# Two small loads on another queue, other PSUM banks for one step's scores, and twenty identity transposes at the start of a fused attention and MLP kernel

## The chip, the cores and the metric

The kernel runs on one core of a Trainium2 chip. The metric is device time in microseconds (us) of one launch, lower is better; the time of a version is the median of several runs.

## The reference

Attention with a threshold, then an MLP with a squared ReLU, all in fp32. What matters of it:

```python
q, k, v: (8, 8, 576, 64)    tau = 0.02    w_in: (512, 2048)   w_out: (2048, 512)
scores = 0.125 * np.matmul(q, k.transpose(0, 1, 3, 2))
thresh = np.max(scores, axis=-1, keepdims=True) - tau
scores = np.where(scores >= thresh, scores, -1000000000.0)
scores = scores - np.max(scores, axis=-1, keepdims=True)
attn = np.exp(scores)
attn = attn / (np.sum(attn, axis=-1, keepdims=True) + 1e-09)
attn_out = np.matmul(attn, v)
x = attn_out.transpose(0, 2, 1, 3).reshape(4608, 512)
h = x @ w_in
r = np.maximum(h, 0.0)
return (r * r) @ w_out
```

## The kernel before, in words

Heads are handled in pairs, because two heads of 64 columns fill the 128 rows of TensorE. A *visit* is one pair of heads of one batch, and a visit is a row of *steps*; a step handles one block of 128 queries of both heads (u = 0 and u = 1). The first visits have two steps each: steps 0 and 1 belong to visit 0, steps 2 and 3 to visit 1, and so on. All engines are scheduled by hand: each engine and each queue does its instructions in the order in which the program writes them. One loop over the steps writes that order, and it spreads pieces of the MLP (attention output times `w_in`, square, times `w_out`) between the attention work of the steps, as soon as enough of the attention output is there. Before that, in the first steps, the attention chain has the engines nearly alone.

At the start, `load_qk(0)` loads the keys and queries of visit 0 in pieces of 32 partitions: four pieces of `kl`, four of `ql`, on the queues of SyncE (SP) and ScalarE (ACT) in turn. Keys m = 2 and m = 3 come in two parts, a large one (16 blocks, L173) and a small one (2 blocks, 8 KB, L175). The small ones are in the same queue as the large one. Then SP issues `load_qk(1)` (into tile `wo`, a part of which serves as a buffer until the weights of the second MLP layer come), the values `load_v(0)` and the first three pieces of weights, `load_weights(0..2)`. The DMAs of SP and ACT share eight completion semaphores in rotation: a ninth one waits until the first has landed, and so on. GpSimd (POOL) meanwhile makes the identity `ident`, issues the load of `tau` (L57), and clears a few tiles (L79, L236). VectorE (DVE) begins with the scaling of `tau` into `ntau8` (L58), and behind it in its order are the transposes `prep(0)` of L226 that make `qT` and `kT` from `ql` and `kl`.

One step s then consists of:

- `scores(s)`: TensorE multiplies `qT` by `kT` (L247), four matmuls of 288 columns (each two records in the trace), two for each head, into the PSUM tiles `s0` and `s1` (two banks each); DVE takes the row maxima (L269, two instructions).
- `turn(s - 2, ...)`: nine transposes on TensorE (L326) turn the finished weights of the step two before, three into one of the four tiles `bank4` to `bank7` (one PSUM bank each); ScalarE copies each three out to `wT` (L327).
- `exponents(s)`: ScalarE makes bias and threshold (L277, L278) and two exponentials out of `s0` and `s1` (L280).
- in the last step of a visit `prep` of the next visit: `qT` and `kT` again (L226, DVE); in other steps DVE has parts of the rounding of a weight piece (L140, L141, L144).
- `mix(...)`: from step 3 on, the weights `wT` times the values (L428).
- `threshold(s)`: DVE compares the scores with the threshold and multiplies (L292, two instructions), then sum and reciprocal (L294, L295).
- `divide(s)`: GpSimd scales the weights (L300, L302).

Every step takes its scores from the same `s0` and `s1`:

```python
sc = [psum.tile([P, 2, 512], FP32, tag=f"s{u}", name=f"s{u}") for u in range(n)]
```

So the matmuls of step s may begin when `threshold(s - 1)`, the last reader of `s0` and `s1`, is done with each of them. The four tiles of `bank` are first used by `turn(0, ...)` in step 2.

Of the kernel before, what the change touches and what calls it, by code (L numbers as in the profile page):

```python
# [9 lines left out]
FP32 = mybir.dt.float32  # L10
U32 = mybir.dt.uint32
AF = mybir.ActivationFunctionType
ALU = mybir.AluOpType
# [6 lines left out]
def kernel(  # L20
# [10 lines left out]
    nc = tc.nc  # L31
    B, H, S, D = q.shape
    d_model, d_ff = moe_w_in.shape
    n_tokens = out.shape[0]
    P = 128
# [10 lines left out]
    SCALE = 0.125  # L46
# [5 lines left out]
    psum = ctx.enter_context(tc.tile_pool(name="psum", bufs=1, space=bass.MemoryType.PSUM))  # L52

    ident = const.tile([P, P], FP32, name="ident")
    make_identity(nc, ident)
    ntau8 = const.tile([P, 1], FP32, name="ntau8")
    nc.gpsimd.dma_start(out=ntau8, in_=tau.to_broadcast([P, 1]))  # L57
    nc.vector.tensor_scalar(out=ntau8, in0=ntau8, scalar1=-1.0 / SCALE, scalar2=None, op0=ALU.mult)  # L58

    w_in_sb = const.tile([P, NMC, d_ff], FP32, name="w_in_sb")  # L60

# [14 lines left out]

    vs = [const.tile([P, 2 * NBLK + 2, D], FP32, name=f"vs{i}") for i in range(2)]
    qmid = const.tile([P, P], FP32, name="qmid")
    nc.gpsimd.memset(qmid, 0.0)  # L79
    at = RAW * 2 * WP  # L80
    w_slots = [const.tile([P, 2, S], FP32, name=f"w{i}") for i in range(2)]
    w_slots.append(spare[:, at:at + 2 * S].rearrange("p (u k) -> p u k", u=2))
# [16 lines left out]
    p5s = const.tile([P, HD], FP32, name="p5s")  # L99
    u_sum = const.tile([P, HD], FP32, name="u_sum")  # L100
    osb = const.tile([P, 2, d_model], FP32, name="osb")
    bank = {i: psum.tile([P, 512], FP32, tag=f"bank{i}", name=f"bank{i}") for i in range(4, 8)}


    n_in = d_ff // WP * NMC
# [18 lines left out]
    def load_weights(i):  # L124
        nc.sync.dma_start(out=weight_area(i).bitcast(mybir.dt.int64), in_=weight_piece(i)[0])
# [25 lines left out]
    def rows_of(n):  # L151
        return rows_in[n % 2 if n <= 2 * HP else 0]
# [3 lines left out]
    def rows_32(t, n, m):  # L156

        b, h = divmod(visits[n][0], HP)
        return t[b, 2 * h + m // 2, :, (m % 2) * 32:(m % 2) * 32 + 32].rearrange("(c p) d -> p c d", p=32)

    def load_qk(n):


        if by_dma(n):
            load_part(k, n)
            load_part(q, n)
            return
        for x, t in ((rows_of(n)[1], k), (rows_of(n)[0], q)):
            for m in range(4):
                src, to = rows_32(t, n, m), x[m * 32:(m + 1) * 32, :, :]  # L170
                queue = nc.scalar if n == 0 and m % 2 else nc.sync
                last = REST // 32 if t is k and m >= 2 else 0
                queue.dma_start(out=to[:, last:, :], in_=src[:, 0:S // 32 - last, :])  # L173
                if last:
                    queue.dma_start(out=to[:, 0:last, :], in_=src[:, S // 32 - last:, :])  # L175

    def load_part(t, n):
        x = rows_of(n)[0 if t is q else 1]
        loads.extend((x[m * 32:(m + 1) * 32, :, :], rows_32(t, n, m)) for m in range(4))
# [31 lines left out]
    def prep(n):  # L211

        prep_part(q, n)
        prep_part(k, n)
# [8 lines left out]
    def prep_part(t, n):  # L223
        to, rows = (qT, rows_of(n)[0]) if t is q else (kT[n % 2], rows_of(n)[1])
        arrived(rows)
        nc.vector.transpose(to, rows.rearrange("p c d -> p (c d)"))  # L226
# [5 lines left out]
    LITTLE = 2.0 ** -20  # L232

    stats = [const.tile([P, 8, 2], FP32, name=f"st{i}") for i in range(4)]
    for st in stats:
        nc.gpsimd.memset(st[:, 4, :], S * LITTLE)  # L236
    weights = {}

    def scores(s):


        vis, i = steps[s]
        n = 2 if i < NBLK or paired(vis) else 1
        sc = [psum.tile([P, 2, 512], FP32, tag=f"s{u}", name=f"s{u}") for u in range(n)]

        def term(u, half, rows, lhsT, keys, to=slice(0, P)):
            nc.tensor.matmul(sc[u][to, half, 0:HALF], lhsT, keys[rows, half * HALF:(half + 1) * HALF],  # L247
                             start=True, stop=True)

        if i == NBLK and paired(vis):  # L250
            for half in range(2):
                for v_ in range(2):
                    for u in range(2):
                        rows, cols = slice(u * D, (u + 1) * D), slice(v_ * D, (v_ + 1) * D)
                        term(u, half, rows, qmid[rows, cols], kT[v_], cols)
        elif i == NBLK:
            for half in range(2):
                term(0, half, slice(0, P), qmid, kT[vis % 2])
        else:
            halves = [(half, u) for half in range(2) for u in range(n)]  # L260
            if early():
                halves.sort(key=lambda x: x[1])
            for half, u in halves:
                rows = slice(u * D, (u + 1) * D)
                term(u, half, rows, qT[rows, i * P:(i + 1) * P], kT[vis % 2])
        st = stats[s % len(stats)]
        mx = st[:, 0, 0:n]
        for u in range(n):
            nc.vector.tensor_reduce(out=mx[:, u:u + 1], in_=sc[u][:, :, 0:HALF], axis=AX.XY, op=ALU.max)  # L269

        w = w_slots[(s - first_dma) % (2 if by_dma(vis) else 3)][:, 0:n, :]
        weights[vis, i] = w, sc, st

    def exponents(vis, i):
        w, sc, st = weights[vis, i]
# [305 lines left out]
    def paired(n):  # L581

        return n >= 3 * HP
# [8 lines left out]
    def by_dma(n):  # L592

        return n >= 3 * HP - 1
# [31 lines left out]
    def early():  # L626
        return state["step"] < min(chunk_at)
# [10 lines left out]
    def add_chunk(j):  # L638
        waiting.extend(pieces_of(j))
# [40 lines left out]
    for s, (n, i) in enumerate(steps):  # L680
        if s < HP * FIRST:
            x = int(n > 0 and i == 0)
        else:
            x = 2 if n >= 2 * HP and i == NBLK else 1
# [46 lines left out]
            prep_at[d].append(lambda n=nxt: prep_part(k, n + 1))  # L731

    load_qk(0)
    load_qk(1)
    load_v(0)
    for i in range(RAW):
        load_weights(i)
    prep(0)
    done = 0
    rounded_by = [0]  # L740
    for s in range(END + 1):
        state["step"] = s
        state["usable"] = rounded_by[-1]
        rounded_by.append(state["rounded"])
        on = s < NST
        now = []
        if on:
            n, i = steps[s]
            at = visits[n][1].index(i)
            last = at == len(visits[n][1]) - 1  # L750
            now = list(range(done, done + pieces[s]))
            done += pieces[s]
            more = n + 1 < len(visits)
            short = n < 2 * HP
            if short and at == 0 and 0 < n + 1 < 2 * HP:
                load_qk(n + 2)
            elif not short and at == 1 and not by_dma(n):
                load_qk(n + 1)
            if now:
                round_weights(now[0], 0)  # L760
            scores(s)
        old = steps[s - 2] if 2 <= s < NST + 2 and not by_dma(steps[s - 2][0]) else None
        at_once = now or old or early()
        lay = on and last and more and not by_dma(n)
        if old:
            turn(*old, 0)
            turn(*old, 1)
        if on:
            exponents(n, i)
            if at == 1:  # L770
                split_left(n)
            if lay:
                prep(n + 1)
            elif now:
                round_weights(now[0], 1)
        if s in mixes and not old:
            mix(*mixes[s])
            for j in chunk_at.get(s, ()):
                add_chunk(j)
        quarter = rate(s) / 4 if s < END else 1e9  # L780
        fill(quarter)
        if s in mixes and old:
            mix(*mixes[s])
            for j in chunk_at.get(s, ()):
                add_chunk(j)
        if old:
            turn(*old, 2)
        state["free"] = s > first_dma
        if on:
            threshold(n, i)  # L790
            for fn in prep_at[s] + load_at[s]:
                fn()
            if lay and now:
                round_weights(now[0], 1)
            if now:
                round_weights(now[0], 2)
                round_weights(now[0], 3)
            if not at_once:
                divide(n, i)
        if 0 < s <= NST and by_dma(steps[s - 1][0]):  # L800
            m, x = steps[s - 1]
            turn_blocks(m, x)
        for what in place_at[s]:
            place_blocks(*what)
        some_loads()
        fill(quarter)
        some_loads()
        if on and at_once:
            divide(n, i)
        fill(quarter)  # L810
        some_loads()
        fill(quarter)
        some_loads()
        if on:
            if now:
                end_rounding(now[0])
            for p in now[1:]:
                for stage in range(4):
                    round_weights(p, stage)
                end_rounding(p)  # L820
            if at == 0 and 0 < n <= 2 * HP:
                load_v(n)
            elif last and n >= 2 * HP and not by_dma(n):
                load_v(n + 1)
# [35 lines left out]
```

## Time and profile before

| | |
|---|---|
| median of 7 runs | 1414.63 us (1411.81 to 1415.89) |
| the profiled execution's own time | 1411.81 us |
| its span, first to last instruction | 1410.0 us |
| TensorE busy | 1359.4 us, 96% of the span |
| VectorE, GpSimd, ScalarE busy | 856.8, 924.4, 439.9 us |
| first matmul of step 0 starts | 8.49 us |
| first matmul of steps 1, 2, 3 starts | 14.29, 20.29, 26.95 us |

The times in the rows of the profile count from the first instruction. PE is TensorE's matmul side, PEld its weight loads, and a name with a q behind it (SPq, POOLq, DVEq) is the sequencer of an engine, which issues DMAs and waits on semaphores. `s<-kT,qT` means that tile `s` is written from `kT` and `qT`. PEclk is the share of its full clock that TensorE was granted. Lines such as L247 are lines of the kernel before.

### The profile page before, as it was taken

How to read it: one execution, taken by the hardware profiler on the slowest of the kernel's cores; microseconds unless marked ns; L12 is line 12 of the kernel's file. 1: busy time of each engine (PE TensorE's matmuls, PEld its weight loads, DVE VectorE, ACT ScalarE, POOL GpSimd, SP SyncE). 2: the span in 40 equal slices, each digit the busy share in tenths (PEclk: the TensorE clock that was granted, in tenths of full speed). 3: DMA queues.
4: the chain of work that ended last, by engine and by line, in shares of the span. 5: the costliest groups of instructions: out<-in, count | busy, mean ns of one | idle time of the engine just before them, and what ended most of it. 6: DMA issues, size and time to landing. Idle time of an engine off the chain costs nothing.

```text
span 1410.0 us, 22712 instructions
## 1 busy us (share of the span) xinstructions
PE 1359.4 (96%) x7556; PEld 1039.9 (74%) x7556; DVE 856.8 (61%) x1898; ACT 439.9 (31%) x1068; POOL 924.4 (66%) x1239
## 2 busy tenths in 40 slices
PE   5898989999999999999999999999999999999998
PEld 3676555767787777777777877777777877788887
DVE  5888886766767676766575766666666666501001
ACT  3776655223232323222222222222222222210110
POOL 2688878777677767777776858585868665422332
PEclk9999999999999999999999999999999999999999
DMA  7664431336555555554535455544445544310000
GB/s 152 133 143 113 130 102 44 64 65 123 97 122 99 117 97 108 95 107 87 108 81 113 98 112 95 101 85 100 91 101 95 120 85 96 64 39 16 1 16 15
DMA packets 397605, 127.95 MB, mean 91 GB/s; under 512 B 379952, under 2 KB 386288, under 8 KB 397488
## 3 DMA queue, kind: packets, MB, share of 16 engines
q1 hardware_dynamic: 373936, 93.01, 35.0%
q0 software_dynamic: 21168, 33.19, 8.7%
q8 instruction: 61, 1.00, 0.3%
q10 hardware_dynamic: 2384, 0.30, 0.1%
q14 instruction: 56, 0.46, 0.1%
HBM read 50.59 MB, written 9.44 MB: 43 GB/s over the span
## 4 chain that ended last, share of the span: by engine, by line
PE 87%; DVE 5%; POOL 2%; ACT 2%; issue 2%; DMA 1%; POOLq 0%; ACTq 0%; DVEq 0%; SPq 0%
PE bank L476 34%; PE bank L543 28%; PE s L247 12%; PE bank L428 10%; DVE st L269 1%; PE bank L326 1%; DVE turned L141 1%; PE bank L510 1%; DVE w L292 1%; ACT w L280 1%; ACT wT L327 1%; POOL g L487 1%; POOL w L302 0%; POOL gsum L466 0%; DVE turned L140 0%
## 5 line engine op out<-in xcount | busy, mean ns | idle before, releaser
L476 PE MATMUL bank<-xT,w_in_sb 128*128 128x256 f32 x2304 | 519.8, 383 | 2.1 <-ACT osb L517 2.1
L476 PEld LDWEIGHTS bank<-xT,w_in_sb 128*128 128x128 f32 x2304 | 432.5, 190 | 82.9 <-issue 22.3
L269 DVE TENSOR_REDUCE st<-s 128x1 f32<-128x576 f32 x288 | 205.7, 752 | 230.0 <-PE s L247 229.8
L292 DVE SCALAR_TENSOR_TENSOR w<-s,st,w 128x576 f32<-128x576 f32 x269 | 209.2, 815 | 112.1 <-ACT w L280 111.9
L543 PE MATMUL bank<-wo,gsum 128*128 128x256 f32 x1088 | 252.7, 385 | 6.0 <-POOL gsum L466 6.0
L302 POOL TENSOR_SCALAR w<-w,st 128x576 f32<-128x576 f32 x269 | 225.0, 844 | 24.7 <-DVE st L295 18.2
L543 PEld LDWEIGHTS bank<-wo,gsum 128*128 128x128 f32 x1088 | 204.1, 191 | 48.9 <-issue 12.5
L487 POOL TENSOR_TENSOR g<-g 128x512 f32<-128x512 f32 x144 | 151.8, 1055 | 114.4 <-ACT g L486 113.1
L277 ACT ACTIVATE st<-st 128x2 f32<-128x2 f32 (+1 forms) x148 | 30.3, 205 | 600.0 <-DVE st L269 599.4
L247 PE MATMUL s<-kT,qT 64*128 64x288 f32 x1024 | 174.7, 438 | 30.6 <-DVE w L292 15.3
L543 PE MATMUL bank<-wo,g 128*128 128x256 f32 x816 | 187.5, 382 | 0.0
L280 ACT ACTIVATE w<-s,st 128x576 f32<-128x576 f32 x269 | 183.3, 732 | 0.4 <-ACT st L278 0.2
L366 DVE STREAM_TRANSPOSE turned<-w 128x512 f32<-128x512 f32 (+2 forms) x388 | 168.8, 489 | 13.8 <-DMA wT<-turned 13.0
L543 PEld LDWEIGHTS bank<-wo,g 128*128 128x128 f32 x816 | 153.4, 190 | 28.4 <-issue 6.4
L428 PE MATMUL bank<-wT,vs 128*64 128x128 f32 (+7 forms) x1700 | 168.6, 357 | 3.1 <-ACT wT L327 2.6
L300 POOL TENSOR_SCALAR st<-st 128x2 f32<-128x2 f32 (+1 forms) x148 | 34.9, 236 | 207.7 <-DVE w L292 197.3
L247 PEld LDWEIGHTS s<-kT,qT 64*128 64x128 f32 x1024 | 98.2, 190 | 90.9 <-issue 62.0
L428 PEld LDWEIGHTS bank<-wT,vs 128*64 128x64 f32 (+1 forms) x1700 | 95.7, 137 | 77.5 <-issue 25.7
L486 ACT ACTIVATE g<-bank 128x512 f32<-128x512 f32 x144 | 86.1, 600 | 176.9 <-PE bank L476 175.9
L190 POOL DMA_DIRECT2D vs<-in_v_dram x144 | 90.9, 635 | 0.0
L557 DVE TENSOR_TENSOR gsum<-g 128x512 f32<-128x512 f32 x34 | 22.9, 704 | 110.6 <-PE bank L543 110.6
L190 POOL DMA_DIRECT2D kl<-in_k_dram x100 | 68.8, 691 | 0.0
(73 smaller groups left out, 1020.6 us busy)
## 6 DMA issues: line engine op xcount, KB each, us to landing
wT<-turned SPq DMA_DIRECT2D x800, 72.0 KB, 2.3
out_dram<-osb POOLq DMA_DIRECT2D x34, 256.0 KB, 2.8
wo<-in_moe_w_in_dram SPq DMA_DIRECT2D x16, 512.0 KB, 4.6
wo<-in_moe_w_out_dram SPq DMA_DIRECT2D x16, 512.0 KB, 3.7
kl<-in_k_dram POOLq DMA_DIRECT2D x100, 72.0 KB, 3.0
ql<-in_q_dram POOLq DMA_DIRECT2D x100, 72.0 KB, 2.7
wT<-turned SPq DMA_DIRECT2D x192, 36.0 KB, 2.2
vs<-in_v_dram POOLq DMA_DIRECT2D x50, 128.0 KB, 3.1
```

Of the source, the lines that this page charges most:

```text
L190: nc.gpsimd.dma_start(out=to, in_=src)
L247: nc.tensor.matmul(sc[u][to, half, 0:HALF], lhsT, keys[rows, half * HALF:(half + 1) * HALF], start=True, stop=True)
L269: nc.vector.tensor_reduce(out=mx[:, u:u + 1], in_=sc[u][:, :, 0:HALF], axis=AX.XY, op=ALU.max)
L280: nc.scalar.activation(out=w[:, u, :].rearrange("p (h k) -> p h k", h=2), in_=sc[u][:, :, 0:HALF], func=AF.Exp, bias=bias[:, u:u + 1], sca ...
L292: nc.vector.scalar_tensor_tensor(out=wu, in0=sc[u][:, :, 0:HALF], scalar=thr[:, u:u + 1], in1=wu, op0=ALU.is_ge, op1=ALU.mult, accum_out=s ...
L302: nc.gpsimd.tensor_scalar(out=w[:, u, :], in0=w[:, u, :], scalar1=z[:, u:u + 1], scalar2=rcp[:, u:u + 1], op0=ALU.add, op1=ALU.mult)
L366: nc.vector.transpose(wb[:, at:at + k1 - k0, i % 2, :], w[:, u, k0 * 32:k1 * 32].rearrange("p (k q) -> p k q", q=32))
L428: nc.tensor.matmul(ps[u * D:(u + 1) * D, :], vs[n % 2][rows, u * (NBLK + 1) + c, :], wT[rows, NBLK if c == NBLK else u * (NBLK + 1) + c, a ...
L476: nc.tensor.matmul(h[:, x % 2, :], w_in_sb[:, c, f * P:(f + 1) * P], xT[:, c, at:at + TCH], start=(c == 0), stop=(c == NMC - 1))
L486: nc.scalar.activation(out=to, in_=h, func=AF.Relu)
L487: nc.gpsimd.tensor_tensor(out=to, in0=to, in1=to, op=ALU.mult)
L543: nc.tensor.matmul(to, left[:, f, :], wo[:, slot, f, :], start=(f == 0), stop=(f == HF - 1))
```

## The change

Five edits that belong together:

1. The two small loads of keys of visit 0 are issued by GpSimd's queue instead of SP's and ACT's (the first instructions of GpSimd after the start).
2. The making of `ident`, the load of `tau` with its scaling, and the clearing of `qmid` and of the four `st` tiles come after `load_qk(0)` in the program, in the same order among themselves. On GpSimd they thereby follow the two small loads; on DVE the order stays.
3. Step 1's scores go to two new tiles `second[0]` and `second[1]` of two banks each, in the four banks that `bank4` to `bank7` take afterwards. All other steps keep `s0` and `s1`.
4. At step 2 the pool of `second` is closed and `bank4` to `bank7` are made in its place, so the first writes to them wait for the last readers of `second`.
5. Twenty TensorE transposes of `ident` into `second[1]` are the first instructions of TensorE; they wait only for `ident`.

The order of everything else on each engine is as before.

```diff
     ident = const.tile([P, P], FP32, name="ident")
-    make_identity(nc, ident)
     ntau8 = const.tile([P, 1], FP32, name="ntau8")
-    nc.gpsimd.dma_start(out=ntau8, in_=tau.to_broadcast([P, 1]))
-    nc.vector.tensor_scalar(out=ntau8, in0=ntau8, scalar1=-1.0 / SCALE, scalar2=None, op0=ALU.mult)
...
-    nc.gpsimd.memset(qmid, 0.0)
...
-    bank = {i: psum.tile([P, 512], FP32, tag=f"bank{i}", name=f"bank{i}") for i in range(4, 8)}
+    startup = ExitStack()
+    spsum = startup.enter_context(tc.tile_pool(name="spsum", bufs=1, space=bass.MemoryType.PSUM))
+    second = [spsum.tile([P, 2, 512], FP32, name=f"second{u}") for u in range(2)]
+    bank = {}
...
                 queue.dma_start(out=to[:, last:, :], in_=src[:, 0:S // 32 - last, :])
                 if last:
+                    queue = nc.gpsimd if n == 0 else nc.sync
                     queue.dma_start(out=to[:, 0:last, :], in_=src[:, S // 32 - last:, :])
...
-    for st in stats:
-        nc.gpsimd.memset(st[:, 4, :], S * LITTLE)
...
-        sc = [psum.tile([P, 2, 512], FP32, tag=f"s{u}", name=f"s{u}") for u in range(n)]
+        sc = [second[u] if s == 1 else psum.tile([P, 2, 512], FP32, tag=f"s{u}", name=f"s{u}")
+              for u in range(n)]
...
+    def keep_busy(times):
+
+        for x in range(times):
+            nc.tensor.transpose(second[1][:, 1, x % 4 * P:x % 4 * P + P], ident, ident)
...
     load_qk(0)
+    make_identity(nc, ident)
+    nc.gpsimd.dma_start(out=ntau8, in_=tau.to_broadcast([P, 1]))
+    nc.vector.tensor_scalar(out=ntau8, in0=ntau8, scalar1=-1.0 / SCALE, scalar2=None, op0=ALU.mult)
+    nc.gpsimd.memset(qmid, 0.0)
+    for st in stats:
+        nc.gpsimd.memset(st[:, 4, :], S * LITTLE)
     load_qk(1)
     load_v(0)
     for i in range(RAW):
         load_weights(i)
     prep(0)
+    keep_busy(20)
...
         state["step"] = s
         state["usable"] = rounded_by[-1]
+        if s == 2:
+            startup.close()
+            bpsum = ctx.enter_context(tc.tile_pool(name="bpsum", bufs=1, space=bass.MemoryType.PSUM))
+            bank.update((x, bpsum.tile([P, 512], FP32, tag=f"bank{x}", name=f"bank{x}")) for x in range(4, 8))
```

## The prediction

> **What bounds the kernel now.** I read the page's busy rows first, then the chain of waits of the first 35 us, then the timeline of the queues, and last the windows of TensorE's clock.
>
> ```profile
> PE 1359.4 (96%) x7556; PEld 1039.9 (74%) x7556; DVE 856.8 (61%) x1898; ACT 439.9 (31%) x1068; POOL 924.4 (66%) x1239
> ...
> PE   5898989999999999999999999999999999999998
> ```
>
> TensorE is the bound of the span; only the first slice (35 us) is half empty. The change touches nothing behind step 2, so what it can give lies in that slice, and a microsecond won there moves all that follows, because everything later waits for what came before it in the program and not for an absolute time. The chain of waits there:
>
> ```profile
> 4.97 2.75 DMA wo<-in_k_dram
> 7.71 0.74 DVE kT L226
> ...
> 8.49 2.30 PE s L247 x8
> ...
> 12.66 0.64 ACT w L280
> ...
> 13.32 0.84 DVE w L292 x2
> ...
> 14.29 2.27 PE s L247 x6
> ...
> 16.59 0.78 DVE st L269 x2
> ...
> 18.77 0.66 DVE kT L226
> 19.43 0.72 DVE wo L292 x2
> ...
> 20.29 2.99 PE s L247 x8
> ...
> 25.98 0.84 DVE w L292 x2
> ...
> 26.95 2.99 PE s L247 x8
> ```
>
> Each step's scores (L247) start 0.14 us after a threshold (L292): the PSUM tiles come free then. Steps 1, 2, 3 start at 14.29, 20.29, 26.95. Step 2 needs two things, the keys of visit 1 (kT done at 19.43) and the tiles of step 1 (from 20.15). The next view, the windows of 3.41 us (busy time of each engine, PEclk third from the end), is for the clock:
>
> ```profile
> core 0: us, PE busy (x) PEld busy (x) DVE busy (x) ACT busy (x) POOL busy (x), PEclk, DMA share, GB/s
> 13.89:17.31 3.42, 2.99 (x8) 1.90 (x8) 2.04 (x7) 0.03 (x1) 1.87 (x3) 1.00 0.72 214
> 20.72:24.13 3.41, 3.41 (x13) 2.36 (x13) 2.04 (x7) 0.15 (x1) 1.84 (x3) 1.00 0.77 117
> 24.13:27.55 3.42, 1.31 (x9) 0.99 (x9) 2.54 (x6) 2.79 (x7) 0.00 (x0) 1.00 0.63 101
> 27.55:30.96 3.41, 3.41 (x12) 2.36 (x11) 2.38 (x6) 0.14 (x1) 2.31 (x4) 0.50 0.86 184
> ...
> 34.37:37.79 3.42, 3.42 (x36) 2.41 (x35) 2.26 (x8) 2.99 (x8) 1.85 (x3) 1.00 0.43 68
> ```
>
> PEclk says 0.50 from 27.55 to 34.37 and 1.00 around it. Before 24.13 its 1.00 cannot be right: eight score records take 2.30 us at 8.49 and 1.25 us at 34.57 (L247 in TensorE's timeline), and transposes start 0.213 us apart up to 24.13 and 0.110 us apart after it. So TensorE is slow until 24.13, fast for one window, slow for two, and fast from 34.37. The clock changes on a grid of 3.41 us that is not tied to the kernel.
>
> **The change part by part.** Estimates are made from these rows, against the profiled execution (own time 1411.81, span 1410.0).
>
> *Two small loads to GpSimd's queue.* The last query piece landed just before 7.00 (timeline of the start):
>
> ```profile
> 1.48 0.70 POOL L57 DMA_DIRECT2D ntau<-in_tau_dram  x1 [0.16 <-issue]
> ...
> 2.26 1.57 SPq L173 DMA_DIRECT2D ql<-in_q_dram  x2
> ...
> 2.34 1.82 ACTq L173 DMA_DIRECT2D ql<-in_q_dram  x2
> ...
> 4.99 0.15 DVE L58 TENSOR_SCALAR ntau<-ntau 128x1 f32<-128x1 f32 x1 [4.99 <-DMA ntau<-in_tau_dram]
> ...
> 7.00 0.78 DVE L226 STREAM_TRANSPOSE qT<-ql 128x576 f32<-128x576 f32 x1 [1.85 <-DMA ql<-in_q_dram]
> ```
>
> With ten loads on eight semaphores, the last two query loads wait for the first two key loads and go out at 3.5 and 3.85. With eight loads none waits: they go out by about 2.4 and, DMAs being busy all along, land near 6.0 (the pieces land 0.3 us apart). SP's later loads (visit 1, values, weights) come about 1.1 us earlier (first one at 3.5 instead of 4.62). But on GpSimd the identity and tau now stand behind two DMA issues of 0.70 each: tau's issue moves from 1.48 to about 2.88, and with its 3.5 us to landing to 6.36. DVE does tau first, so the query transpose starts at about 6.55 instead of 7.00, kT is done at 8.0, scores start at 8.05: **-0.44**. Tau is late next, not the queries; each microsecond more of it costs one. The GpSimd loads of keys land near 4.3 and 5 by the same row, before kT needs them (7.25). The clearings on GpSimd end near 4, and GpSimd has nothing else until 14.98: free. ACT is relieved of one issue.
>
> *Twenty transposes.* `ident` is ready at 0.74 + 1.40 + 0.58 = 2.75; at 0.213 they end near 7.0, a microsecond before the scores: in nobody's way (if kT came before 7.0 they would delay it). What they are worth depends on the clock. The Trainium skill ("TensorE: Matmul & The Clock Gate", Part 4: PE-mode transpose) speaks against them: a transpose does not count as busy for the clock gate. This trace says otherwise. I weigh each record by the share of the array that it fills (a score record 64 of 128 rows, a half) and its spacing: the windows from 7.07 and 13.89 are filled to 0.53 and 0.56 and the clock stays low, 20.72 to 24.13 to 0.75, of which 0.25 are transposes, and it rises; 27.55 to 30.96 to 0.68, it does not rise. Without its transposes the window that raised it would have 0.50, less than one that did not. So they count, and about 0.7 of a window is needed. Twenty make 4.3 us without a gap: at most phases of the grid (about four in five) one window is full enough before the scores end. The clock falls after a window filled to 0.31 or less (from 24.13: 0.26; from 235.76: 0.31) and holds at 0.35 (from 133.36), so scores of step 0 mostly still find it: 1.25 instead of 2.30, **-1.05**. By the skill's rule it would be 0. I take the trace. Over the 6 us without matmuls up to step 2 the clock is lost again.
>
> *Step 1's scores in other banks.* They follow step 0's on TensorE at once, finished long before DVE can read them. DVE's own work then sets step 1. Before, from the end of step 0's maxima (12.25) to kT of visit 1 (19.43): 7.18 us. After: exponentials and thresholds with L294, L295 until 15.35, 3.10 us; two maxima 1.50; qT and kT 1.43: 6.03. **-1.15**. The loads of visit 1 landed by 11.6 here and are earlier now.
>
> *Step 2* finds `s0` and `s1` free since step 0, so it starts with kT and both heads run together: 0.04 + 2.30 at low clock, instead of 0.86 + 2.99. Its maxima end 3.8 after kT. The first transposes of `turn(0)` now also wait for step 1's threshold (1.55 after kT, the shared banks), while step 2's scores run until 2.35: hidden, 0 (at a high clock the wait would show with 0.3). Six transposes and two copies on ACT then end 4.25 after kT, L277, L278 and the exponential 1.1 later: threshold 2 at 5.35 after kT instead of 6.55 (25.98 - 19.43). **-1.2**.
>
> From step 3 on order and waits are as before. Sum: -0.44 - 1.05 - 1.15 - 1.2 = **-3.8 us** in the profiled execution. What remains is the low clock from 27.55 to 34.37, where TensorE was busy without a pause from 26.95 to 34.64. Whether it gets the clock a window sooner or later is the grid's accident, worth up to about 1.5 us either way, before and after alike. Adding the same durations along the chain for each phase of the grid gives a typical gain of 3.6 to 4.4. I take 4.0. The profiled execution is the fastest of the seven and 2.8 below the median, so I set the sum against the median: 1414.63 - 4.0 = **1410.6**.
>
> A later taker would have to be SP: a visit there is some 18 loads at 0.54, about 9.7 us of the 10.6 of two steps. It gets only 1.1 us ahead while the chain gains 4. But queries of visit 2 were issued by 22.6 and landed by 24.7; about 23.6 now, and needed at about 26 (30.66 before). Values of visit 1 then land near 34, needed near 37.5. Margins of 2.5 and 3.5 us: free, but the next to break.
>
> **The rivals.**
>
> *Transposes do not raise the clock* (the skill's rule). For it: no window of transposes alone is in this trace. Then -2.8 to -3.3: about 1411.6.
>
> *The start is held by GpSimd's queue.* Tau or the small key loads land 1 to 2 us later than I put them, since the trace has only one early load of that queue, from a quieter time, and DMA share is near 1 from 5 to 7. Between no delay and one in which tau lands behind all query loads: gain 1.5 to 3, about 1412.5.
>
> *The gain is taken back*: loads by SP are late at visit 2 or weights at their rounding. Gain 0 to 2: about 1413.6.
>
> *Slower*: the same queue, but far later. DVE is in order, so tau's multiply holds every transpose. The other parts give 3.4; slower than before by 0.2% needs scores at 8.49 + 3.4 + 2.8 = 14.7, tau at about 13, so two issues of some 4 us each instead of 0.70. Against it: no DMA issue on GpSimd in the page's groups has a mean over 0.70 us. It would be about 1418. That the edit does nothing is excluded for the banks: step 1's wait for the threshold is gone from the instruction order.
>
> **How the numbers follow.** A difference under 0.2% (2.8 us, about what a measurement of this kernel can tell from none) counts as the same: 1411.8 to 1417.5. As summed: 0.57, all faster. Low clock: 0.15, faster in 0.09, the same in 0.06. GpSimd late: 0.12, faster in 0.03, the same in 0.09. Taken back: 0.08, the same. Slower: 0.08. Faster 0.69, same 0.23, slower 0.08. The range, 1407.6 to 1413.6, takes in the clock's grid and the first three rivals in most of their width.
>
> **What would show it.** Right: scores of steps 0, 1, 2, 3 start at about 8.05, 9.1, 16.7 and 22.8; step 0's eight records take about 1.25; qT's transpose follows the tau multiply at once near 6.5; steps from 5 on lie 4 us earlier than 39.34 and the end as much. Wrong: score records of step 0 still 0.48 us apart (clock); tau landing after 7.5 (queue); a shift at 40 us that is gone at 300 us (taken back).

## The result, and the profile after

The median of 14 runs is 1410.59 us (1408.32 to 1413.68), against 1414.68 for before in 34 runs: a ratio of 0.997, with a 95% interval of 0.9962 to 0.9977. That is 4.1 us, faster by 0.3%. Run again later beside other kernels, its ratio was 0.9977 (0.9968 to 0.9986). The profiled execution took 1408.90 us with a span of 1407.1, 2.9 under the profiled one of before.

The page's busy rows of the kernel after:

```profile
PE 1360.6 (97%) x7576; PEld 1043.6 (74%) x7576; DVE 854.9 (61%) x1898; ACT 439.9 (31%) x1068; POOL 924.2 (66%) x1241
...
PE   6898988999999999999999999999999999999998
```

TensorE has twenty records more and the same busy time within 1.2 us; only the first slice is fuller. The chain of waits of its first 35 us (start, duration, what):

```profile
8.19 0.75 DVE kT L227
...
8.98 1.25 PE s L247 x8
...
10.26 1.43 DVE st L269 x2
...
12.76 1.57 DVE w L297 x4
...
15.36 0.75 DVE st L269
16.11 0.69 DVE qT L227
16.79 0.67 DVE kT L227
...
17.60 2.30 PE s L247 x8
...
21.40 0.48 ACT wT L332
...
22.84 0.84 DVE w L297 x2
...
23.81 2.06 PE s L247 x7
25.86 1.48 PE bank L331 x6
```

From step 0's threshold (12.76) to the keys of visit 1 (17.46) the chain now runs on DVE alone: the threshold, the maxima of step 1 and the two transposes follow each other, and no score of step 1 is waited for. Step 2's scores start 0.14 after kT, with no threshold in between. Step 3 starts at 23.81 instead of 26.95. But the first scores start at 8.98, later than the 8.49 of before. The timeline of the start:

```profile
1.34 1.26 POOL L176 DMA_DIRECT2D kl<-in_k_dram  x2 [0.88 <-POOLq L858]
...
3.13 0.59 POOL L740 DMA_DIRECT2D ntau<-in_tau_dram  x1
...
3.24 4.53 PE L277 MATMUL second<-ident 128*128 128x128 f32 x20 [3.24 <-POOL ident masks.py:199]
...
7.31 0.15 DVE L741 TENSOR_SCALAR ntau<-ntau 128x1 f32<-128x1 f32 x1 [7.31 <-DMA ntau<-in_tau_dram]
7.49 0.78 DVE L227 STREAM_TRANSPOSE qT<-ql 128x576 f32<-128x576 f32 x1
```

GpSimd's first load starts at 1.34, tau's at 3.13, and DVE waits for tau until 7.31 before it turns the queries.

### The profile page after: what moved, and what is told of

Read it like the earlier page. It is cut to its first block, busy times and chain, and to the rows that moved or that the text cites. A ratio compares the mean times of both kernels' runs of the same rounds, so it can differ in the third digit from the quotient of the medians.

```text
span 1407.1 us, 22756 instructions
## 1 busy us (share of the span) xinstructions
PE 1360.6 (97%) x7576; PEld 1043.6 (74%) x7576; DVE 854.9 (61%) x1898; ACT 439.9 (31%) x1068; POOL 924.2 (66%) x1241
## 4 chain that ended last, share of the span: by engine, by line
PE 88%; DVE 5%; ACT 3%; POOL 2%; issue 1%; DMA 1%; POOLq 0%; ACTq 0%; DVEq 0%; SPq 0%
PE bank L481 35%; PE bank L548 28%; PE s L247 12%; PE bank L433 10%; DVE turned L141 1%; PE bank L331 1%; PE bank L515 1%; DVE st L269 1%; ACT wT L332 1%; DVE w L297 1%; ACT w L285 1%; POOL g L492 0%; DVE turned L140 0%; POOL gsum L471 0%; DVE wo L297 0%
## 5 line engine op out<-in xcount | busy, mean ns | idle before, releaser
L247 PE MATMUL s<-kT,qT 64*128 64x288 f32 x1016 | 170.8, 435 | 23.5 <-DVE w L297 13.0
L146 POOL TENSOR_TENSOR turned<-turned 128x512 f32<-128x512 f32 x32 | 41.1, 1286 | 43.1 <-DVE turned L144 42.7
```

## The experiments

| kernel | median, us | ratio to before beside it | first scores at, us | their eight records, us | step 3 starts at, us |
|---|---|---|---|---|---|
| changed | 1410.59 | 0.997 (0.9962 to 0.9977) | 8.98 | 1.25 | 23.81 |
| without transposes | 1411.24 | 0.997 (0.9955 to 0.9985) | 9.04 | 2.30 | 24.91 |
| banks only | 1411.70 | 0.9968 (0.9953 to 0.9982) | 8.44 | 2.30 | 24.31 |
| loads only | 1414.49 | 0.9989 (0.9973 to 1.0005) | 9.37 | 2.30 | 28.06 |
| tau behind | 1410.27 | 0.9958 (0.9941 to 0.9975) | 8.87 | 1.25 | 23.69 |
| ten transposes | 1412.76 | 0.9979 (0.9968 to 0.999) | 9.15 | 2.30 | 25.02 |
| bridged | 1408.82 | 0.9957 (0.9942 to 0.9973) | 8.51 | 1.25 | 22.86 |
| fewer queries, visit 0 | 1409.08 | 0.9959 (0.9947 to 0.9972) | 7.83 | 1.25 | 22.65 |
| fewer queries, all | 1409.29 | 0.9957 (0.9942 to 0.9972) | 7.69 | 1.25 | 22.18 |
| matmuls | 1413.04 | 0.9979 (0.9969 to 0.9989) | 8.95 | 1.25 | 23.77 |
| fewer queries, bridged | 1409.62 | 0.9961 (0.9949 to 0.9974) | 7.70 | 1.76 | 22.57 |
| changed, again | 1412.13 | 0.9977 (0.9968 to 0.9986) | 8.99 | 2.30 | 24.86 |

The kernels ran in four groups, each beside its own runs of before: the first row, the next four, the four from "ten transposes" to "fewer queries, all", and the last three. Before had medians of 1414.7, 1415.4, 1415.9 and 1415.0 in them, and the last three groups ran on three different chips, so medians are compared within a group and ratios across groups. The intervals of most of these ratios overlap, so what separates the parts is the start of each profiled execution, not the median.

**The parts of the change, one by one.** Without the transposes:

```diff
-    keep_busy(20)
```

> The changed kernel without its twenty transposes; all else as changed. My theory (transposes raise TensorE's clock for the first scores): the first eight score records take 2.3 us instead of the 1.25 of the changed kernel, the scores of steps 2 and 3 start about 1.0 us later than 17.60 and 23.81, the median is about 1.0 us above that of the changed kernel (some 1411.6). Rival (a transpose does not count for the clock, so they give nothing): the first eight take what they take in the changed kernel and the median is the same within 0.5 us. The first scores start at 8.98 as there (tau decides, not TensorE).

```profile
9.04 2.30 PE L247 MATMUL s<-kT,qT 64*128 64x288 f32 x8 [9.04 <-DVE kT L227]
```

The first eight records took 2.30 us and step 3 started 1.10 later than in the changed kernel, as expected. The ratio to before is 0.997, the same as with the transposes. So they work in the trace; that they pay in the median is not shown.

The banks alone (the `second` tiles and their closing at step 2, put into the kernel before):

```diff
-        sc = [psum.tile([P, 2, 512], FP32, tag=f"s{u}", name=f"s{u}") for u in range(n)]
+        sc = [second[u] if s == 1 else psum.tile([P, 2, 512], FP32, tag=f"s{u}", name=f"s{u}")
+              for u in range(n)]
...
```

> The kernel before with only step 1's scores in the other four banks (no load moved, no transposes). My theory (the banks carry most of the gain, by letting DVE run from step 0's threshold straight to step 1's maxima and by freeing step 2): first scores at 8.49, keys of visit 1 done about 1.2 us sooner than 19.43, threshold of step 2 about 5.4 us after them instead of 6.55, so scores of step 3 some 2.4 to 2.6 us sooner than 26.95; median 2.5 to 3.5 us under that of before. Rival (most of it comes from the clock at the start): less than 1.5 us under it.

The chain of waits of this kernel:

```profile
10.77 1.43 DVE st L274 x2
...
17.30 0.67 DVE kT L230
...
18.10 2.30 PE s L252 x8
...
23.34 0.84 DVE w L297 x2
```

Keys of visit 1 are done at 17.97 instead of 19.43, step 2's threshold 5.37 later (23.34) instead of 6.55, and step 3 starts 2.64 sooner. The median is 3.7 under before. The rival, that most of it comes from the clock at the start, fell: the first scores are as slow here as before. With a ratio of 0.9968 the banks alone reach what the whole change reaches (0.997), so in the median they account for the gain; what the other parts add to it is not resolved.

The loads alone (the changed kernel without `second` and without `keep_busy`):

> The changed kernel's move of the two small loads and of identity, tau and the clearings alone; scores in the old banks, no transposes. My theory (tau's load now stands behind two loads on GpSimd's queue, and DVE waits for it ahead of its first transpose): first scores at about 9.0 instead of 8.49, so this part alone costs 0.5 us: the median 0 to 1 us above that of before. Rival (the step of the prediction, the queries' earlier landing counts): first scores at about 8.05, median 0.4 us under it.

```profile
7.69 0.15 DVE L737 TENSOR_SCALAR ntau<-ntau 128x1 f32<-128x1 f32 x1 [7.69 <-DMA ntau<-in_tau_dram]
7.87 0.78 DVE L224 STREAM_TRANSPOSE qT<-ql 128x576 f32<-128x576 f32 x1
```

In DVE's timeline tau's multiply waits until 7.69, the query transpose follows at once, and the scores start at 9.37, 0.88 later than before. The trace shows the loss; the median (ratio 0.9989, interval up to 1.0005) does not. As an addition to the start, this part costs; the prediction had it as a gain.

**What holds the first scores.** My theory was that it is tau. One line moves:

```diff
-    nc.vector.tensor_scalar(out=ntau8, in0=ntau8, scalar1=-1.0 / SCALE, scalar2=None, op0=ALU.mult)
...
     prep(0)
+    nc.vector.tensor_scalar(out=ntau8, in0=ntau8, scalar1=-1.0 / SCALE, scalar2=None, op0=ALU.mult)
     keep_busy(20)
```

> The changed kernel with DVE's scaling of tau put behind the first two transposes in its order (one line moved). My theory (tau's landing at 7.29 holds the transposes, the queries are there at 5.97): the query transpose starts at about 6.0, the key transpose at about 6.8, the first scores at about 7.6 to 7.8 instead of 8.98; the median 1.0 to 1.4 us under that of the changed kernel, about 1409.4, the lowest so far. The twenty transposes end at about 7.8, so they may hold the first scores by a few tenths. Rival (something else, such as the keys that GpSimd loads, holds them just as long): first scores at 8.8 or later and no change of the median.

```profile
7.38 0.78 DVE L227 STREAM_TRANSPOSE qT<-ql 128x576 f32<-128x576 f32 x1 [7.38 <-DMA ql<-in_q_dram]
8.08 0.74 DVE L227 STREAM_TRANSPOSE kT<-kl 128x576 f32<-128x576 f32 x1
8.74 0.11 DVE L749 TENSOR_SCALAR ntau<-ntau 128x1 f32<-128x1 f32 x1
```

That fell. With tau out of the way, DVE waits for the queries, until 7.38, and the scores start at 8.87. The bridged kernel below has the same order on DVE, and its queries came sooner:

```profile
7.01 0.78 DVE L227 STREAM_TRANSPOSE qT<-ql 128x576 f32<-128x576 f32 x1 [7.01 <-DMA ql<-in_q_dram]
```

Its scores start at 8.51. So moving tau alone brought 0.1 us in one profile and 0.5 in the other, by the landing of the last query piece (7.18 and 6.81). The expectation rested on queries that were there at 5.97; that was the landing of the second of four pieces. The last one lands at 6.93 in the changed kernel, at 6.98 before. The DMA view of the changed kernel's first 8 us shows why (busy tenths of the DMA engines in 40 slices; then queue, count, size of each, median from issue to landing):

```profile
DMA  0000000005799999999999999999999999999731
...
ql<-in_q_dram SPq DMA_DIRECT2D x2, 72.0 KB, 4.1
ql<-in_q_dram ACTq DMA_DIRECT2D x2, 72.0 KB, 4.4
...
ntau<-in_tau_dram POOLq DMA_DIRECT2D x1, 0.5 KB, 4.1
```

Before, the same view has 3.2 and 3.3 for the queries and 3.5 for tau. The last two pieces are issued 1.3 and 1.5 us earlier, and take that much longer. From 2 us on the DMA engines are busy all the time in this view, so my reading was that the bytes ahead of a load decide when it lands. SP's loads of visit 1 also go out sooner (3.78 instead of 4.62) and share the engines; what they take from the last queries was not separated. The next experiment tries fewer bytes, with the query rows that steps 0 and 1 read (8 of the 18 blocks of 32 rows) loaded and turned alone:

```diff
+                if t is q and n == 0:
+                    part = used_blocks(n)
+                    queue.dma_start(out=to[:, part, :], in_=src[:, part, :])
+                    continue
...
+        if t is q and n == 0:
+            part = used_blocks(n)
+            nc.vector.transpose(to[:, part.start * 32:part.stop * 32],
+                                rows[:, part, :].rearrange("p c d -> p (c d)"))
+            return
...
```

> The changed kernel, but for visit 0 only the 256 query rows that its two steps read are loaded and transposed (of 576). My theory (the DMA engines are full from 2 us on, so the last query piece lands at 6.94 no matter when it is issued, and tau behind it at 7.29; what counts is the bytes ahead of it): 164 KB less at about 150 GB/s bring tau and the last queries 1.0 to 1.1 us sooner, near 6.2; the query transpose takes 0.42 instead of 0.78; the first scores start at 7.6 to 7.8 instead of 8.98, held perhaps by the twenty transposes that end at 7.8; median 1.0 to 1.4 us under that of the changed kernel. Rival (tau's landing is the latency of GpSimd's queue, 4.15 us after its issue whatever the load): tau at 7.3 still, first scores at 8.6.

```profile
6.49 0.15 DVE L755 TENSOR_SCALAR ntau<-ntau 128x1 f32<-128x1 f32 x1 [6.49 <-DMA ntau<-in_tau_dram]
6.67 0.45 DVE L238 STREAM_TRANSPOSE qT<-ql 128x256 f32<-128x256 f32 x1
7.04 0.73 DVE L241 STREAM_TRANSPOSE kT<-kl 128x576 f32<-128x576 f32 x1
```

Tau lands at 6.46 instead of 7.28, the last queries at 6.09 instead of 6.93: 0.8 us for the 164 thousand bytes less, somewhat under the 1.0 to 1.1 expected. Tau was issued at 3.13, as in the changed kernel, so its landing is not a fixed latency, and the rival fell. The two later kernels with fewer queries agree (last queries at 6.06 and 6.13). The scores start at 7.83, and the twenty transposes, which end at 7.76, are now as late as the keys.

For all eight short visits (condition `n < 2 * HP` instead of `n == 0`, tau behind):

> The same for all eight short visits (256 or 320 of 576 query rows), with tau's scaling behind the first two transposes. My theory as for fewer queries at visit 0, and 0.35 us more at step 1, where the transposes of visit 1 stand on the chain; later ones stand beside ScalarE's work and give little: first scores at 7.5 to 7.8, keys of visit 1 done at about 15.8 (17.46 in the changed kernel), median 1408.5 to 1409.3. Rival (they are on the chain at every short visit): 0.35 us at each of seven, the median near 1407.

First scores at 7.69, step 2's at 15.97. From the eighth step (51.4 us in before's profile) on it lies 5.01 us ahead of before, and 103 us in before's profile still finds it 5.05 ahead: later visits give nothing, as expected. There DVE's transposes stand beside ScalarE's work: in the profile of before, those of visit 2 run from 30.66 to 32.09, and DVE then still waits 0.82 for an exponential. The median is 1409.29.

**The clock.** The edges of the clock's windows of 3.41 us, its grid, fall differently from profile to profile. A window's fill is worked out as in the prediction: the time that its records stream, times the share of the array that they use, over 3.41 us. Half of the transposes:

```diff
-    keep_busy(20)
+    keep_busy(10)
```

> The changed kernel with ten transposes at the start instead of twenty. My theory (the clock rises only after a window of its 3.41 us grid that is filled to about 0.74; ten at 0.213 us make 2.1 us, at most 0.62 of a window): the clock does not rise before the scores, so the first eight score records take 2.3 us and the median is that without transposes, about 1411.2 to 1411.6. Rival (any activity just before, or the fetch of TensorE's first instructions, is what makes the first scores quick): 1.25 us, and the median of the changed kernel.

The windows of this kernel on its grid, then those of the changed kernel (behind the length of the window PE busy, PEclk third from the end):

```profile
2.12:5.54 3.42, 2.31 (x10) 2.00 (x10) 0.00 (x0) 1.28 (x1) 1.87 (x9) 1.00 1.39 165
5.54:8.95 3.41, 0.08 (x1) 0.00 (x0) 1.45 (x3) 0.00 (x0) 0.00 (x0) 1.00 0.94 114
```

```profile
5.04:8.45 3.41, 2.73 (x13) 2.33 (x11) 1.11 (x3) 0.00 (x0) 0.00 (x0) 1.00 1.11 125
8.45:11.86 3.41, 2.31 (x16) 1.68 (x16) 1.90 (x3) 0.15 (x2) 0.00 (x0) 1.00 0.63 115
15.28:18.69 3.41, 1.09 (x5) 0.92 (x7) 3.41 (x7) 2.55 (x6) 1.32 (x2) 0.50 0.96 347
18.69:22.10 3.41, 3.32 (x15) 2.16 (x11) 2.64 (x8) 1.39 (x6) 1.85 (x3) 0.50 0.97 160
22.10:25.52 3.42, 1.71 (x8) 1.29 (x8) 2.89 (x9) 1.70 (x4) 0.18 (x1) 1.00 0.76 121
25.52:28.93 3.41, 3.41 (x23) 2.72 (x22) 2.54 (x5) 2.03 (x6) 3.24 (x5) 0.50 0.78 129
28.93:32.34 3.41, 3.41 (x25) 2.30 (x21) 2.92 (x8) 2.46 (x6) 2.51 (x4) 1.00 0.81 212
```

PEclk is again not to be believed before its first change in a trace, and the durations are: in the repeated run below it shows 1.00 right ahead of scores of 2.30 us. In the changed kernel the window from 5.04 held nothing but transposes. The last one started at 7.35 and streamed for 0.21, so 2.52 of the 3.41 us were filled, 0.74, and the scores behind it took 1.25. By 15.28 the clock is down, as a window without matmuls lies in between; the full window from 18.69 brings it back, the one from 22.10 (filled to 0.27) loses it.

With ten, the window from 2.12 was filled to 0.63 (ten times 0.213) and the first scores took 2.30. This run alone places no bound: the window behind it, from 5.54, was all but empty and, by the same pattern, would have lost the clock again before 9.15. The repeated run of the changed kernel decides:

> The changed kernel itself once more, as the mark for the other two on this chip. Both theories: first scores near 9.0, held by tau's landing at 7.3 or later, a ratio to before of 0.997; the first score records 1.25 us where a window of the grid before them was filled to about 0.74 by the transposes, 2.3 us where not (about one phase in four).

```profile
3.23 4.53 PE L277 MATMUL second<-ident 128*128 128x128 f32 x20 [3.23 <-POOL ident masks.py:199]
8.99 2.30 PE L247 MATMUL s<-kT,qT 64*128 64x288 f32 x8 [1.23 <-DVE kT L227]
```

```profile
5.22:8.64 3.42, 2.54 (x12) 2.14 (x11) 1.29 (x3) 0.00 (x0) 0.00 (x0) 1.00 0.95 116
```

The same twenty transposes from the same moment, but its grid lay so that the windows from 1.81 and 5.22 were filled to 0.57 and 0.68 (the second is the line above; 2.34 of its 2.54 us are streaming), and the first scores took 2.30. For windows of transposes alone the bound lies between 0.68 and 0.74. For windows of scores and transposes together the working is rougher: those from 16.97 with tau behind and from 17.03 with matmuls also come to about 0.74, and the clock stayed at 0.50. Of the eight profiles with twenty records at the start (the matmuls below included), six had first scores of 1.25 us, one of 1.76 (the clock rose during them), one of 2.30.

Ten fp32 matmuls of the identity in the place of the twenty transposes:

```diff
-            nc.tensor.transpose(second[1][:, 1, x % 4 * P:x % 4 * P + P], ident, ident)
+            nc.tensor.matmul(second[1][:, 1, x % 4 * P:x % 4 * P + P], ident, ident, start=True, stop=True)
...
-    keep_busy(20)
+    keep_busy(10)
```

> The changed kernel with ten fp32 matmuls of the identity (two records each, so again twenty of 128 columns) in the place of its twenty transposes. My theory (for the clock a transpose counts like a matmul): they take the same time from the same start, 4.1 to 4.5 us from 3.24, raise the clock as the transposes do, first score records 1.25 us, median that of the changed kernel within 1 us. Rival (the page on TensorE: a transpose does not count as a matmul does): matmuls raise the clock a window sooner or more often, the median 0.5 us or more lower.

They took 4.18 us from 3.23, and the scores 1.25. The grid lay there as with tau behind (edges at 6.79 and 6.74), where transposes gave 1.25 as well: in the trace, no difference between the two. The median is 0.9 above that of the changed kernel beside it; the intervals of the two ratios (0.9969 to 0.9989 and 0.9968 to 0.9986) are the same.

The gap of 6 us before step 2 was then filled with transposes into columns that no score uses, in the kernel with tau behind the transposes of DVE:

```diff
+        if s == 1:
+            bridge(28)
         st = stats[s % len(stats)]
...
+        if s == 1:
+            bridge(10)
         w = w_slots[(s - first_dma) % (2 if by_dma(vis) else 3)][:, 0:n, :]
...
+    def bridge(times):
+
+        for x in range(times):
+            nc.tensor.transpose(second[1][:, x % 2, 512 - P:512], ident, ident)
```

> The kernel with tau's scaling behind the transposes, and 38 more identity transposes on TensorE in the gap between the scores of step 1 and step 2 (28 before step 1's maxima, 10 behind them), to columns of the second bank that no score uses. My theory (fill of the clock's windows decides, transposes count, and the gap of 6.3 us is what loses the clock again): the clock stays high until step 2, whose score records take 1.25 instead of 2.3 us; the first scores of step 3 start about 0.8 us sooner after the keys of visit 1 than the 6.3 of the changed kernel; by step 5 1 to 2 us are won; median 1408.5 to 1409.5. Rival (a clock raised there does not help, since DVE and ACT set the pace): step 2's scores quick, but no more than 0.3 us won. Risk: where the grid leaves the clock low, 28 transposes take 6 us and delay step 1's maxima by 1 to 2 us.

Step 2's scores took 1.25 us. Part of the gain went into a new wait, which its chain shows:

```profile
15.69 1.32 PE second L286 x10
...
17.03 0.75 ACT wo L294
...
17.81 0.84 DVE wo L306 x2
```

The last ten transposes write the tile that step 1's exponentials read, so ScalarE waits for them and step 1's threshold starts 9.30 us after the first scores, 0.9 later than in the changed kernel (17.37 - 8.98). Step 3 starts 14.35 after the first scores, instead of 14.83 in the changed kernel. It won 0.5 us there, less than the 0.8 expected. The median of 1408.82 is the lowest of all, but its ratio (0.9957) is that of tau behind without a bridge (0.9958), so that the bridge pays in the median is not shown.

Fewer queries at all short visits and the bridge together, beside the repeated run:

> Fewer query rows for all eight short visits, tau's scaling behind the transposes, and the 38 transposes that bridge the gap to step 2, together. My theory (the two act on different terms and add up): first scores at 7.7 to 7.8, step 2's scores at about 16.0 and in 1.25 us, step 3's some 0.7 us before the 22.18 of fewer queries alone, median 1407.5 to 1408.8, 2 us under the changed kernel on the same chip. Rival (the bridge was a matter of the grid's phase and gives nothing beside fewer queries): the median of fewer queries alone, about 1409.3.

1409.62, 2.5 under the changed kernel beside it. They did not add up in this profile: its grid left the clock low into the first scores (1.76 us), and step 3 starts at 22.57, later than with fewer queries alone. So the five versions with tau behind or fewer queries have ratios of 0.9957 to 0.9961 against 0.997 and 0.9977 of the changed kernel, some 1 to 3 us better, with intervals that overlap; which of them is best is not resolved.

**Where several microseconds come and go later.** From step 5 up to about 100 us every profile of the table below keeps its lead within 0.4 us, and then it changes until 290 us, where windows at low clock lie. By the maxima of the steps, against before:

| kernel | ahead of before at 103 us | at the end | us at low clock from 100 to 300 us (before: 10.2) | phase of the grid against the program |
|---|---|---|---|---|
| changed | 4.33 | 2.87 | 13.7 | 2.5 |
| bridged | 5.29 | 3.85 | 13.7 | 2.6 |
| fewer queries, all | 5.05 | 3.61 | 13.7 | 2.5 |
| without transposes | 2.25 | -2.61 | 20.5 | 2.2 |
| banks only | 3.91 | -1.71 | 23.9 | 2.4 |
| fewer queries, visit 0 | 4.54 | -0.03 | 23.9 | 2.2 |

The last column says how the grid lies against the program at 103 us: the place of an edge plus the lead, counted round in 3.41 us. The profiles near 2.5 have the same low windows in the same places (about 134, 196 and 285 us) and lose the same 1.4 us; those near 2.2 to 2.4 have others, near 111 and 132 besides, and lose 4.6 to 5.6. Two different kernels, that with tau behind and that with matmuls, whose grids happened to lie alike (edges at 6.74 and 6.79 us), have all their low windows within 0.1 us of each other and end at spans of 1409.6 and 1409.7. Each us at low clock more than before cost between 0.33 and 0.48 in these six, and between 0.33 and 0.69 in the other six. All twelve lose against the profile of before, which was the fastest of its first seven runs. So much of the spread of single runs by some 5 us goes with this phase, and a comparison of two spans is one of two phases. That the phase causes it is not shown: it was not tried to hold the phase fixed.

## Why the prediction was right, and where its steps were not

The forecast was 1410.6 and the median is 1410.59. The agreement is better than its steps. The scores of steps 0 to 3 were put at 8.05, 9.1, 16.7 and 22.8 and started at 8.98, 10.06, 17.60 and 23.81. Of these the 22.8 does not follow from the prediction's own terms: 26.95 less their 3.84 is 23.11.

*Two small loads to GpSimd's queue, -0.44.* This step failed, in its sign: scores start 0.49 later. Two terms were wrong. "They go out by about 2.4 and, DMAs being busy all along, land near 6.0" does not follow from its own reason: while the DMA engines are busy, an earlier issue need not land earlier, and the last queries land at 6.93, as before (6.98). Tau was put at 6.36 and landed at 7.28. GpSimd's first issue started at 1.34, not 0.74, so tau went out at 3.13 instead of 2.88; the larger part is the landing, which took 4.15 instead of 3.5. That tau is late next was right in the changed kernel, but the queries land only 0.35 us before it, so taking tau away alone brought 0.1 and 0.5. This was the rival of a start held by GpSimd's queue, in part.

*Twenty transposes, -1.05.* The size is exact where the grid let it happen: 2.30 to 1.25. The choice of the trace against the rule of the Trainium skill ("TensorE: Matmul & The Clock Gate", Part 4: PE-mode transpose) held: by the rule the first scores would have stayed at 2.30, but a window of transposes alone raised the clock, and matmuls in their place did no more. The fill needed is nearer 0.74 than 0.7, so 20 are just enough, at some phases not: `ident` was ready at 3.2, not 2.75 (the terms given add up to 2.72), and the transposes ended at 7.77, not 7.0. (The window from 27.55, put at 0.68, comes nearer 0.72 by the starts of its records; it did not raise the clock.)

*Step 1's other banks, -1.15.* 7.18 us became 5.77 (11.69 to 17.46), so -1.41: the time up to L295 is the 3.10 of the sum, and the rest is shorter because DVE's instructions overlap (the maxima of step 1 start at 14.70, the reciprocal before them ends at 14.79).

*Step 2, -1.2.* kT to threshold took 5.38, predicted 5.35: -1.17.

Together -3.14 at step 3 instead of -3.84. The typical gain of 3.6 to 4.4 over the phases, from which the 4.0 came, cannot be redone from what is shown. What was left to "the grid's accident" then gave 1.2 in this profile: by step 5 it lies 4.29 ahead, and the chain stays there. The median, which averages over phases, came out at 4.1. Since the first step was put 0.93 too good and the others 0.23 too low, part of that agreement is luck: the repeated run, in which no window before the first scores was full enough, was 2.05 ahead at the same place and its median is 2.9 under before.

*The gain taken back by SP* did not happen: the leads at step 5 and at 103 us differ by no more than 0.4 us in every profile of the table above, and the latter is never the smaller.

## What to carry to other kernels

Before moving a load forward, see whether the DMA engines are already busy between its issue and its landing; if they are, an earlier issue may bring no earlier landing (6.93 instead of 6.98 here), and fewer bytes ahead of it may (6.09). Loading only the rows that the first steps read started the first scores at 7.83, against 8.98 with the reordering alone. At the start of a chain, a second set of buffers for one step is worth what the last reader of the first set makes the next step wait, counted on the engine that carries the chain. Where single runs differ by more than the effect, read the effect where it is made in the trace, and compare ends only between runs that had the same clock windows.

## What the runs showed of the hardware that was not expected

- A window of 3.41 us that held only identity transposes, filled to 0.74, raised TensorE's clock (scores 2.30 to 1.25 us); in the repeated run of the same kernel, one filled to 0.68 did not.
- The first DMA issue on GpSimd's queue, when it is the first instruction behind the start, began at 1.34 us, while SP and ACT issued at 0.75.
- A load of 0.5 KB lands later the more is ahead of it on the DMA engines: tau landed 3.5 us after an issue at 1.48, 4.15 us after one at 3.13 behind all queries, and 3.3 us after one at 3.13 with 164 thousand bytes of queries less ahead.
